# Threshold attention followed by an ELU feed-forward block: the heads of one stage in two PSUM tiles, each with its own maximum and with its bound on ScalarE

## The chip, the core and the metric

The kernel runs on one core of a Trainium2 chip. The core has five engines, each of which takes its instructions in order: TensorE (PE in the profile; its weight loads are listed apart as PEld), VectorE (DVE), ScalarE (ACT), GpSimd (POOL) and SyncE (SP, which issues the DMAs here). The metric is the device time of one execution in microseconds (us), as the median of several runs.

## The reference

Everything is float32, except that the two weight matrices arrive as 64-bit floats and are brought to 32 bits by the kernel. Cut to what matters:

```python
# q, k, v: (8, 8, 576, 64); tau = 0.02
scores = scale * np.matmul(q, k.transpose(0, 1, 3, 2))          # scale = 1/8
thresh = np.max(scores, axis=-1, keepdims=True) - tau
scores = np.where(scores >= thresh, scores, -1000000000.0)
scores = scores - np.max(scores, axis=-1, keepdims=True)
attn = np.exp(scores)
attn = attn / (np.sum(attn, axis=-1, keepdims=True) + 1e-09)
x = np.matmul(attn, v)                                          # heads side by side: (4608, 512)
h = x @ w_in                                                    # (512, 2048)
g = np.where(h > 0.0, h, np.exp(np.minimum(h, 0.0)) - 1.0)
out = g @ w_out                                                 # (2048, 512)
```

## The kernel before

**Attention in steps.** Two heads form a pair; there are 32 pairs, `pr` = 0 to 31, four to a batch. A pair is worked through in five steps, `i` = 0 to 4: steps 0 to 3 each take 128 of the 576 query rows for both heads, step 4 takes the 64 rows left over of both heads together as one tile of 128 rows ("one-head step"). Steps are counted through as n = 5 pr + i. One step consists of these parts:

- `scores` (L238): PE multiplies queries by keys into PSUM. For each half of the 576 keys (`a`) and each head (`h`) there is a matmul; the loop order is a outside, h inside. A head's scores take two PSUM banks of 288 columns each.
- `exponentials`: VectorE takes the row maximum `mx` from PSUM (L248); GpSimd makes `nb`, the maximum times minus the scale (L249), which is the bias of the exponential, and `th`, the maximum less tau in unscaled terms (L250), which is the bound below which scores are dropped; ScalarE makes `e`, the exponential of each head (L253).
- `masks` (L265): VectorE compares the scores in PSUM with `th`, multiplies by `e`, writes `w` to SBUF and sums its rows in `sm`; then it makes the reciprocals `rs` (L267, L268).
- `normalize` (L274): GpSimd multiplies `w` by `rs`.
- the turn: PE transposes `w` into PSUM (`rt`, L277) in two or three parts, and ScalarE copies them to SBUF (`wTa`, `wTb`, L293).
- `values` (L384, L388): after steps 1 and 4 of a pair, PE multiplies by v (`pv`), and ScalarE copies the result out (`xt`, L395, `xs`, L400).

**Four stages.** Steps 0 to 19 are laid out by the framework's scheduler. Steps 20 to 34 (up to `SWITCH`) have an order written out by hand, and carry beside them the conversion of the weights and the first units of the plain feed-forward block. Steps 35 to 44 (up to `MIDDLE`) run beside the rest of the plain feed-forward units, one head at a time in two PSUM tiles. From step 45 on the order comes from a planner with due times, beside a feed-forward block that needs fewer products; this stage has helpers of its own for the parts of a step: `max_of` (L1096), `bound_of` (L1100), `exp_of` (L1104, L1106), `mask_of` (L1115), `reciprocal_of` (L1121, L1122). After the last step only the feed-forward block is left.

**The stage that the change touches, steps 20 to 34.** PSUM holds three pools here: `t` with two banks (transposes and values), `f` with two banks (feed-forward) and `s` with one tile of four banks, which takes both heads of a step. The tile is given back when its masks have been made. The loop issues, in this order:

1. `scores` of step n; `values` of step n - 2 if that was a step 1 or 4 of its pair (then n mod 5 is 3 or 1; the code calls this `valued`);
2. if not `valued`: the first part of converting one weight piece (`convert_top`, two VectorE operations, L136 and L137, and `convert_add` on GpSimd, L143); the exponentials and "minus one" of feed-forward halves carried over;
3. a share of feed-forward halves on PE (`SHARES`: up to one half at each of four places), the first part of the transposes of step n - 1, and, if not `valued`, their copies on ScalarE;
4. `exponentials`; the ELU of carried halves;
5. if `valued`: `convert_top` and `convert_add` of the first piece, then the copies out of `values` and of the transposes;
6. `convert_abs` (ScalarE, L148), more feed-forward halves (L435 or L475, their exponentials L442), the second weight piece, the other transposes;
7. `masks`, "minus one" (L445), `normalize`, `convert_end` (VectorE, L155), the ELUs (VectorE, L449), and what the next pair needs (`prep_q`, L195, `copy_q`, L207, `prep_k`, L200, `copy_k`, L212, loads by SP); `convert_rest` (ScalarE, L129) of the next two pieces.

Two weight pieces are converted in each step as long as there are any. A flag, the list `apart`, tells `scores` whether the two heads share one tile or get one each; it was set after this stage.

Of the kernel before, what the change touches and what calls it, by code (L numbers as in the profile page):

```python
# [10 lines left out]
FP32 = mybir.dt.float32  # L11
U32 = mybir.dt.uint32
I32 = mybir.dt.int32
AF = mybir.ActivationFunctionType
ALU = mybir.AluOpType
AX = mybir.AxisListType
# [3 lines left out]
def kernel(  # L20
# [10 lines left out]
    nc = tc.nc  # L31
    PSUM = bass.MemoryType.PSUM
    P = 128
    B, H, S, D = q.shape
# [4 lines left out]
    HALF = S // 2  # L39
# [14 lines left out]
    att = ctx.enter_context(tc.tile_pool(name="att", bufs=2))  # L54
# [9 lines left out]
    wpool = [wstage]  # L64
# [17 lines left out]
    keep = const.tile([P, 1], FP32, name="keep")  # L82
    nc.vector.tensor_scalar(keep, pos, SCALE, None, ALU.mult)
    nkeep = const.tile([P, 1], FP32, name="nkeep")
# [3 lines left out]
    ntau = const.tile([P, 1], FP32, name="ntau")  # L88
# [129 lines left out]
    wTs, xts, open_steps, turns = {}, {}, {}, {}  # L218
    apart = []
# [24 lines left out]
    def exponentials(pr, i, hs):  # L244
        st = open_steps[pr, i]
        cs = slice(hs[0], hs[-1] + 1)
        src = st["both"] if len(hs) == 2 else st[hs[0]].unsqueeze(1)
        nc.vector.tensor_reduce(st["mx"][:, cs], src[:, :, :, :HALF], axis=AX.XY, op=ALU.max)  # L248
        nc.gpsimd.tensor_scalar(st["nb"][:, cs], st["mx"][:, cs], nkeep, 1.0, ALU.mult, ALU.mult)  # L249
        nc.gpsimd.tensor_scalar(st["th"][:, cs], st["mx"][:, cs], 1.0, ntau, ALU.mult, ALU.add)  # L250
        for h in hs:
            e = att.tile([P, 2, HALF], FP32, name="e")
            nc.scalar.activation(e, st[h][:, :, :HALF], AF.Exp, bias=st["nb"][:, h : h + 1], scale=keep)  # L253
            st[h] = st[h], e

    def masks(pr, i, hs):
        st = open_steps[pr, i]
        cs = slice(hs[0], hs[-1] + 1)
        if hs[0] == 0:
            st["w"] = wpool[0].tile([P, 2 * S], FP32, name="w")  # L260
        w, sm, rs = st["w"], st["sm"], st["rs"]
        for h in hs:
            sc, e = st.pop(h)
            wv = w[:, h * S : (h + 1) * S].rearrange("p (a n) -> p a n", a=2)
            nc.vector.scalar_tensor_tensor(wv, sc[:, :, :HALF], st["th"][:, h : h + 1], e, ALU.is_ge, ALU.mult,  # L265
                                           accum_out=sm[:, h : h + 1])
        nc.vector.tensor_scalar(sm[:, cs], sm[:, cs], 1e-9, None, ALU.add)  # L267
        nc.vector.reciprocal(rs[:, cs], sm[:, cs])  # L268

    def normalize(pr, i, hs):  # L270
        st = open_steps[pr, i]
        for h in hs:
            wv = st["w"][:, h * S : (h + 1) * S]
            nc.gpsimd.tensor_scalar(wv, wv, st["rs"][:, h : h + 1], 1.0, ALU.mult, ALU.mult)  # L274

    def transpose(dst, src):
        nc.tensor.matmul(dst, src, ident, is_transpose=True, skip_group_check=True)  # L277
# [228 lines left out]
    def heads_of(i):  # L506
        return [0, 1] if i < NC else [0]
# [68 lines left out]
        if hs == [1]:  # L576
            ahead(pr, i + 1)
    first.close()
    for name, bufs in (("s", 1), ("f", 2)):
        psum[name] = banks.enter_context(tc.tile_pool(name=f"ps_{name}", bufs=bufs, space=PSUM))  # L580

    while len(turned) > 1:
# [8 lines left out]
    with tc.manual_schedule():  # L591
        carried = []
        for _ in range(2):
            load_w(4)
        for n in range(per_seq, SWITCH):
            pr, i = step = steps[n]
            hs = heads_of(i)
            now = range(progress[1], min(progress[1] + 2, len(pieces)))
            if n == per_seq:
                for x in now:  # L600
                    convert_rest(x)
            for _ in now:
                load_w(4)
            scores(*step, hs)
            valued = steps[n - 2][1] in (1, NB - 1)
            if valued:
                out_values = values(steps[n - 2][0], 0 if steps[n - 2][1] == 1 else 1)
            parts = turn_parts(*steps[n - 1])

            if not valued:  # L610
                for x in now[:1]:
                    convert_top(x)
            finish_units(carried, slice(0, 2))
            if not valued:
                for x in now[:1]:
                    convert_add(x)
            share = SHARES[n % NB]
            early_ = ffn_halves(share[0])
            copies = parts[0]()
            if not valued:  # L620
                copies()
            exponentials(*step, hs)
            finish_units(carried, slice(2, None))
            if valued:
                for x in now[:1]:
                    convert_top(x)
                    convert_add(x)
            if valued:
                out_values()
                copies()  # L630
            for x in now[:1]:
                convert_abs(x)
            finish_units(early_, ACT)
            after = ffn_halves(share[1])
            finish_units(after, ACT)
            after = early_ + after
            for x in now[1:]:
                convert_top(x)
                convert_add(x)
                convert_abs(x)  # L640
            parts[1]()()
            second = ffn_halves(share[2])
            finish_units(second, ACT)
            if len(parts) > 2:
                parts[2]()()
            carried = ffn_halves(share[3])
            masks(*step, hs)
            finish_units(after, slice(1, 2))
            normalize(*step, hs)
            finish_units(second, slice(1, 2))  # L650
            for x in now:
                convert_end(x)
            finish_units(after + second, slice(2, None))
            if i in (2, 3):
                (prep_q if i == 2 else prep_k)(pr + 1)
                (copy_q if i == 2 else copy_k)(pr + 1)
            if i in (3, 4):
                load(pr + 2, ("qm",) if i == 3 else ("km",))
            if i == 3:
                load(pr + 1, ("v",))  # L660
            if steps[n - 2] == (NPAIR - 1, NB - 1):
                push_ffn(0)
            for x in range(progress[1], min(progress[1] + 2, progress[0])):
                convert_rest(x)
        finish_units(carried, ALL)
        turn(*steps[SWITCH - 1])
        finish_units(ffn_halves(len(pending)), ALL)
        behind(*steps[SWITCH - 2])
        behind(*steps[SWITCH - 1])
    assert progress[1] == len(pieces)  # L670
    assert units[0][1][0] == 1 and not pending
    banks.close()
    apart.append(True)
    for name, bufs, stack in (("f", 3, ctx), ("s", 2, banks), ("t", 1, banks)):
        psum[name] = stack.enter_context(tc.tile_pool(name=f"ps_{name}2", bufs=bufs, space=PSUM))
    early.close()
# [80 lines left out]
    with tc.manual_schedule():  # L757
        after = []
        make_out(1), make_out(0)
        for n in range(SWITCH, MIDDLE):  # L760
            pr, i = steps[n]
            hs = heads_of(i)
# [328 lines left out]
                    at(end + lag, f)  # L1091
                n -= 1

        def max_of(pr, i, h):
            st = open_steps[pr, i]
            nc.vector.tensor_reduce(st["mx"][:, h : h + 1], st[h][:, :, :HALF], axis=AX.XY, op=ALU.max)  # L1096

        def bound_of(pr, i, h):
            st = open_steps[pr, i]
            nc.gpsimd.tensor_scalar(st["th"][:, h : h + 1], st["mx"][:, h : h + 1], 1.0, ntau, ALU.mult, ALU.add)  # L1100

        def exp_of(pr, i, h):
            st = open_steps[pr, i]
            nc.scalar.mul(st["nb"][:, h : h + 1], st["mx"][:, h : h + 1], nkeep)  # L1104
            e = att.tile([P, 2, HALF], FP32, name="e")
            nc.scalar.activation(e, st[h][:, :, :HALF], AF.Exp, bias=st["nb"][:, h : h + 1], scale=keep)  # L1106
            st[h] = st[h], e

        def mask_of(pr, i, h):
            st = open_steps[pr, i]  # L1110
            if h == 0:
                st["w"] = wpool[0].tile([P, 2 * S], FP32, name="w")
            sc, e = st.pop(h)
            wv = st["w"][:, h * S : (h + 1) * S].rearrange("p (a n) -> p a n", a=2)
            nc.vector.scalar_tensor_tensor(wv, sc[:, :, :HALF], st["th"][:, h : h + 1], e, ALU.is_ge, ALU.mult,  # L1115
                                           accum_out=st["sm"][:, h : h + 1])

        def reciprocal_of(pr, i, hs):
            st = open_steps[pr, i]
            cs = slice(hs[0], hs[-1] + 1)  # L1120
            nc.vector.tensor_scalar(st["sm"][:, cs], st["sm"][:, cs], 1e-9, None, ALU.add)  # L1121
            nc.vector.reciprocal(st["rs"][:, cs], st["sm"][:, cs])  # L1122

        begun = [0.0]

        def softmax(pr, i):
# [40 lines left out]
        for n in range(MIDDLE, len(steps) + 3):  # L1167
            pr, i = divmod(n, NB)
# [61 lines left out]
        w = wpool[0].tile([P, 2 * S], FP32, name="w")  # L1230
# [8 lines left out]
        a, z = B - 1, B  # L1239
# [45 lines left out]
```

## Time and profile before

| what | value |
|---|---|
| median of 6 runs | 1377.13 us (1375.71 to 1379.39) |
| the profiled execution: its time | 1375.71 us |
| its span, first to last instruction | 1373.9 us |
| mean granted clock of TensorE | 0.992 |
| busy in the span: PE, DVE, POOL, ACT | 97%, 77%, 61%, 46% |
| instructions | 21955 |

A busy time is the time in which the engine had an instruction in work. "Idle before" and the waits are attributed to the instruction that came last of those waited for. Windows are given in us from the start of the span; for each the profile lists the busy time of PE, PEld, DVE, ACT and POOL with the number of instructions, the clock that TensorE was granted as a share of full speed, and the share and rate of the DMA engines. The chain of waits is the work that ended last, followed back from the end: each line gives a start, a duration, and the engine and group, and "issue" is time for which the profile shows no wait.

### The profile page before, as it was taken

What the parts mean: (1) busy time and instruction counts of PE and PEld (TensorE: products, weight loads), DVE (VectorE), ACT (ScalarE), POOL (GpSimd) and SP (SyncE); (2) the same over time, 40 slices, a digit from 0 to 9 for tenths busy, and PEclk for the clock granted to TensorE, in tenths of its full rate; (3) what the DMA queues carried; (4) which work ended last, traced back from release to release, by engine and by line L of the source; (5) the groups of instructions that cost most, each with busy time, mean ns of one, the idle gap of its engine ahead of it and who ended that gap; (6) DMA issues with size and microseconds to landing.
All of it is one profiled execution on the core that took longest, in us unless ns stands there. A gap on an engine that the chain in (4) does not pass through costs nothing.

```text
span 1373.9 us, 21955 instructions
## 1 busy us (share of the span) xinstructions
PE 1331.8 (97%) x6566; PEld 990.1 (72%) x6566; DVE 1060.9 (77%) x2364; ACT 625.3 (46%) x1371; POOL 835.0 (61%) x1345
## 2 busy tenths in 40 slices
PE   6898989999999999999999999999999999999998
PEld 4555745746777777777777777777777777888886
DVE  6778895888879887988799878988888875545433
ACT  4666664225454454545353636364535442312320
POOL 5567774778657574757476747665575646525423
PEclk9999999999999999999999999999999999999999
DMA  5235452589798989898889889897989785321211
GB/s 116 58 84 148 143 145 47 167 241 264 222 244 231 281 218 256 226 263 233 235 234 262 243 232 255 224 260 212 246 230 278 223 241 165 124 68 66 93 58 31
DMA packets 316342, 259.82 MB, mean 189 GB/s; under 512 B 208320, under 2 KB 272320, under 8 KB 316224
## 3 DMA queue, kind: packets, MB, share of 16 engines
q1 hardware_dynamic: 316224, 258.42, 68.0%
q8 instruction: 53, 0.87, 0.3%
q14 instruction: 65, 0.53, 0.1%
HBM read 167.84 MB, written 90.51 MB: 188 GB/s over the span
## 4 chain that ended last, share of the span: by engine, by line
PE 87%; DVE 5%; POOL 2%; ACT 2%; issue 2%; DMA 1%; SPq 1%; DVEq 0%; POOLq 0%; ACTq 0%
PE f L1012 28%; PE f L857 28%; PE sc L238 13%; PE pv L388 9%; PE f L475 3%; PE pv L384 3%; PE f L435 3%; PE rt L277 1%; DVE w L265 1%; ACT e L253 1%; DVE mx L248 1%; POOL wtop L143 1%; POOL w L274 1%; DVE wtop L136 0%; DVE wtop L137 0%
## 5 line engine op out<-in xcount | busy, mean ns | idle before, releaser
L274 POOL TENSOR_SCALAR w<-w,rs 128x576 f32<-128x576 f32 x288 | 247.7, 866 | 108.2 <-DVE rs L1122 74.8
L1096 DVE TENSOR_REDUCE mx<-sc 128x1 f32<-128x576 f32 x207 | 148.0, 752 | 80.6 <-PE sc L238 80.5
L238 PE MATMUL sc<-kT,qT 64*128 64x288 f32 x1024 | 182.4, 440 | 26.8 <-DVE w L265 17.2
L348 DVE STREAM_TRANSPOSE x<-w 128x512 f32<-128x512 f32 (+1 forms) x350 | 182.6, 568 | 8.2 <-POOL w L274 8.2
L1106 ACT ACTIVATE e<-sc,nb,keep 128x576 f32<-128x576 f32 x207 | 172.2, 832 | 6.9
L1115 DVE SCALAR_TENSOR_TENSOR w<-sc,th,e 128x576 f32<-128x576 f32 x207 | 163.2, 811 | 8.5 <-ACT e L1106 0.4
L1104 ACT ACTIVATE nb<-mx,nkeep 128x1 f32<-128x1 f32 x207 | 61.5, 297 | 232.0 <-DVE mx L1096 232.0
L238 PEld LDWEIGHTS sc<-kT,qT 64*128 64x128 f32 x1024 | 100.5, 190 | 91.9 <-issue 52.7
L857 PE MATMUL f<-xt,sw 128*128 128x256 f32 x512 | 128.9, 389 | 0.5 <-DVE g L879 0.5
L857 PE MATMUL f<-xt,w_in_sb 128*128 128x256 f32 x512 | 124.5, 382 | 0.3 <-ACT w L871 0.2
L1100 POOL TENSOR_SCALAR th<-mx,ntau 128x1 f32<-128x1 f32 x207 | 54.7, 266 | 104.7 <-DVE mx L1096 104.4
L857 PEld LDWEIGHTS f<-xt,sw 128*128 128x128 f32 x512 | 93.3, 190 | 29.0 <-issue 13.5
L857 PEld LDWEIGHTS f<-xt,w_in_sb 128*128 128x128 f32 x512 | 96.1, 190 | 18.9 <-ACT xs L400 4.6
L1012 PE MATMUL f<-w_out_sb,s 128*128 128x256 f32 x448 | 109.4, 387 | 0.0
L1012 PE MATMUL f<-w_out_sb,g 128*128 128x256 f32 x448 | 107.5, 382 | 0.5 <-DVE g L912 0.5
L253 ACT ACTIVATE e<-sc,nb,keep 128x576 f32<-128x576 f32 x81 | 65.2, 831 | 92.1 <-POOL nb L249 91.1
L1012 PE MATMUL f<-t,s 128*128 128x256 f32 x448 | 106.6, 380 | 0.3 <-POOL s L949 0.3
L857 PE MATMUL f<-x,w_in_sb 128*128 128x256 f32 x448 | 105.8, 379 | 0.0
L1012 PEld LDWEIGHTS f<-w_out_sb,s 128*128 128x128 f32 x448 | 82.3, 190 | 23.0 <-issue 11.6
L1012 PEld LDWEIGHTS f<-w_out_sb,g 128*128 128x128 f32 x448 | 83.8, 190 | 16.8 <-issue 3.8
L876 POOL TENSOR_TENSOR u<-u,w 128x256 f32<-128x256 f32 x64 | 49.1, 767 | 76.4 <-ACT u L871 76.4
L1012 PEld LDWEIGHTS f<-t,s 128*128 128x128 f32 x448 | 84.1, 190 | 13.7 <-POOL s L949 2.7
(162 smaller groups left out, 2579.3 us busy)
## 6 DMA issues: line engine op xcount, KB each, us to landing
there<-x SPq DMA_DIRECT2D x500, 144.0 KB, 4.3
wTb<-there SPq DMA_DIRECT2D x75, 576.0 KB, 4.8
wTa<-there SPq DMA_DIRECT2D x50, 576.0 KB, 4.4
sw<-win_sums SPq DMA_DIRECT2D x62, 384.0 KB, 4.7
t<-wout_sums SPq DMA_DIRECT2D x45, 512.0 KB, 5.4
qm<-in_q_dram SPq DMA_DIRECT2D x128, 72.0 KB, 4.4
vm<-in_v_dram SPq DMA_DIRECT2D x64, 128.0 KB, 4.3
wst<-in_moe_w_in_dram SPq DMA_DIRECT2D x16, 512.0 KB, 4.5
```

The costliest lines, as they stand in the source:

```text
L238: nc.tensor.matmul(scs[h][:, a, :HALF], qs[r], kT[r, k0 : k0 + HALF], start=True, stop=True)
L253: nc.scalar.activation(e, st[h][:, :, :HALF], AF.Exp, bias=st["nb"][:, h : h + 1], scale=keep)
L274: nc.gpsimd.tensor_scalar(wv, wv, st["rs"][:, h : h + 1], 1.0, ALU.mult, ALU.mult)
L348: nc.vector.transpose(x[:, :, c0 : c0 + nc_], src.rearrange("p (c g n) -> p g c n", c=nc_, n=T))
L388: nc.tensor.matmul(pv[h * D : (h + 1) * D, g0 * T : g1 * T], vm[:, h, c], wT[:, g0:g1, h * (NC + 1) + c], start=False, stop=(c == NC - 1), ...
L857: nc.tensor.matmul(loc["banks"][place], left[:, j], right[:, j], start=(begins and j == 0), stop=(j == 1), skip_group_check=True)
L1012: nc.tensor.matmul(place(m), lhs, rhs, start=(begins and v == 0), stop=(v == RU - 1), skip_group_check=True)
L1096: nc.vector.tensor_reduce(st["mx"][:, h : h + 1], st[h][:, :, :HALF], axis=AX.XY, op=ALU.max)
L1100: nc.gpsimd.tensor_scalar(st["th"][:, h : h + 1], st["mx"][:, h : h + 1], 1.0, ntau, ALU.mult, ALU.add)
L1104: nc.scalar.mul(st["nb"][:, h : h + 1], st["mx"][:, h : h + 1], nkeep)
L1106: nc.scalar.activation(e, st[h][:, :, :HALF], AF.Exp, bias=st["nb"][:, h : h + 1], scale=keep)
L1115: nc.vector.scalar_tensor_tensor(wv, sc[:, :, :HALF], st["th"][:, h : h + 1], e, ALU.is_ge, ALU.mult, accum_out=st["sm"][:, h : h + 1])
```

## The change

In steps 20 to 34 each head gets a PSUM tile of its own: the pool `s` has two tiles of two banks instead of one of four, and the flag `apart` is set ahead of the stage. `exponentials` is replaced there by the three helpers of the last stage, called head by head: a maximum per head on VectorE, `nb` per head on ScalarE right ahead of that head's exponential, and `th` per head on GpSimd. `masks` is replaced by `mask_of` for each head and one `reciprocal_of`. The helpers are moved up in the file so that both stages can call them. The places of the parts in the loop stay as they were, and the stages behind are as they were.

```diff
+    def max_of(pr, i, h):
+        st = open_steps[pr, i]
+        nc.vector.tensor_reduce(st["mx"][:, h : h + 1], st[h][:, :, :HALF], axis=AX.XY, op=ALU.max)
+
+    def bound_of(pr, i, h):
+        st = open_steps[pr, i]
+        nc.gpsimd.tensor_scalar(st["th"][:, h : h + 1], st["mx"][:, h : h + 1], 1.0, ntau, ALU.mult, ALU.add)
+
+    def exp_of(pr, i, h):
+        st = open_steps[pr, i]
+        nc.scalar.mul(st["nb"][:, h : h + 1], st["mx"][:, h : h + 1], nkeep)
+        e = att.tile([P, 2, HALF], FP32, name="e")
+        nc.scalar.activation(e, st[h][:, :, :HALF], AF.Exp, bias=st["nb"][:, h : h + 1], scale=keep)
+        st[h] = st[h], e
+
+    def mask_of(pr, i, h):
+        st = open_steps[pr, i]
+        if h == 0:
+            st["w"] = wpool[0].tile([P, 2 * S], FP32, name="w")
+        sc, e = st.pop(h)
+        wv = st["w"][:, h * S : (h + 1) * S].rearrange("p (a n) -> p a n", a=2)
+        nc.vector.scalar_tensor_tensor(wv, sc[:, :, :HALF], st["th"][:, h : h + 1], e, ALU.is_ge, ALU.mult,
+                                       accum_out=st["sm"][:, h : h + 1])
+
+    def reciprocal_of(pr, i, hs):
...
     first.close()
-    for name, bufs in (("s", 1), ("f", 2)):
+    apart.append(True)
+    for name, bufs in (("s", 2), ("f", 2)):
         psum[name] = banks.enter_context(tc.tile_pool(name=f"ps_{name}", bufs=bufs, space=PSUM))
...
-            exponentials(*step, hs)
+            for h in hs:
+                max_of(pr, i, h)
+                exp_of(pr, i, h)
+                bound_of(pr, i, h)
             finish_units(carried, slice(2, None))
...
-            masks(*step, hs)
+            for h in hs:
+                mask_of(pr, i, h)
+            reciprocal_of(pr, i, hs)
             finish_units(after, slice(1, 2))
             normalize(*step, hs)
...
     banks.close()
-    apart.append(True)
```

More of the change, by code (lines that the diff above doesn't have):

```diff
@@ L274, in normalize @@
             nc.gpsimd.tensor_scalar(wv, wv, st["rs"][:, h : h + 1], 1.0, ALU.mult, ALU.mult)
+    def max_of(pr, i, h):
[19 more added lines that the diff above has]
+    def reciprocal_of(pr, i, hs):
+        st = open_steps[pr, i]
+        cs = slice(hs[0], hs[-1] + 1)
+        nc.vector.tensor_scalar(st["sm"][:, cs], st["sm"][:, cs], 1e-9, None, ALU.add)
+        nc.vector.reciprocal(st["rs"][:, cs], st["sm"][:, cs])
     def transpose(dst, src):
@@ L1092, in ffn_quarters @@
                 n -= 1
[L1094 to L1122, printed above, removed]
         begun = [0.0]
```

## The prediction

> **What bounds the kernel now.** I read the whole span first, then the stage that is edited, then the single steps of it. All times are from the profiled execution of the kernel before (span 1373.9 us). Table of windows over the stage, its parts and what follows (us of the window, then the busy time of each engine, the granted clock, DMA share):
>
> ```profile
> 157.80:166.70 8.90, 8.90 (x54) 5.92 (x53) 8.76 (x17) 6.28 (x14) 6.02 (x7) 1.00 0.37 123
> 192.00:201.40 9.40, 6.46 (x25) 2.93 (x24) 8.01 (x16) 6.97 (x16) 6.43 (x6) 1.00 0.49 125
> 201.40:212.00 10.60, 10.59 (x45) 5.00 (x45) 10.17 (x19) 5.52 (x11) 8.76 (x8) 0.84 0.30 103
> 240.20:1300.00 1059.80, 1056.52 (x5252) 804.61 (x5251) 848.62 (x1898) 470.80 (x1059) 661.83 (x1075) 1.00 0.78 218
> ```
>
> Behind 240.2 PE idles 3.3 us in 1060: what is saved ahead of it should move the rest as a block. The edited stage (steps 20 to 34, from 105.9 to 240.2) has PE busy 118.2 of 134.3, so 16 us of gaps, spread unevenly: some steps are full (157.8), others wait (192.0). At most these 16 us and the time lost to the halved clock are to be had. The waits of that stage say for whom (us in total, times, longest):
>
> ```profile
> ACT e L253 <- POOL nb L249: 27.0, 13, 3.9
> PE sc L238 <- DVE w L265: 13.5, 7, 4.5
> DVE w L265 <- ACT e L253: 13.3, 10, 2.8
> ```
>
> PE's scores wait for the masks (w), the masks for the exponentials (e), these for the bound nb on GpSimd. The chain of waits through step 30 shows how (start, us, engine, group):
>
> ```profile
> 196.28 1.29 POOL wtop L143
> 197.58 0.43 POOL nb L249
> 198.01 0.02 issue
> 198.03 0.62 ACT e L253
> ...
> 198.76 0.83 ACT e L253
> ...
> 199.70 1.57 DVE w L265 x4
> 201.27 0.14 issue
> 201.41 1.24 PE sc L238 x8
> ```
>
> The maxima (L248) had begun at 195.97 and taken 1.35, so they were ready at 197.3, but nb stands in GpSimd's queue behind a weight conversion (wtop L143), then both exponentials run, and only then both masks, since both heads lie in one tile.
>
> **The change part by part.** *Maxima.* One reduce of 1152 columns (mean 1342 ns, 11 rows) becomes two of 576, which the last stage has already (L1096, median 749 ns, a pair back to back 1.40 to 1.42 us). So +0.07 us of DVE for each of the 12 two-head steps, but the first maximum stands 0.6 us earlier. [...]
>
> *Bound nb.* It leaves GpSimd (266 to 450 ns a step, behind L143) for ACT, one per head (L1104, median 295 ns, with the exponential 0.3 us after nb's start: 340.67 to 340.99). ACT takes +0.6 us per two-head step; it is busy 78.6 of 134.3. Behind the two nb on ACT are queued weight absolutes, transposed copies and the FFN's exponentials; they start no later as long as the exponentials end no later. With GpSimd free, before: reduce 1.35, nb 0.4, two exponentials 1.55, some 3.4 us from the first reduce's start; after: 0.75 + 0.3 + 0.83 + 0.3 + 0.83, about 3.1. The lower bound th stays on GpSimd, two small ops for one; in step 30 the first would come at 197.6 and end by 198.3 even at the 0.73 of the contended rows, before its mask wants it.
>
> *Masks, scores, order.* Mask 0 needs only exponential 0, and the next step's head-0 scores only mask 0. In the trace the two heads' matmuls of a step overlap (eight passes of 0.40 in 1.24 us); what head 0 gains by going ahead I price at nothing, since PE stands in order and head 1 still needs its 1.24 us after mask 1. It costs nothing either, as PE idles there. No DMA and no instruction of SP moves.
>
> Now the steps. Steps count i = n mod 5; i = 0, 2, 4 convert the first weight piece ahead of the maxima, i = 1, 3 both pieces between maxima and masks.
>
> Two-head steps that convert first (20, 22, 25, 27, 30): from the reduce's start to the first mask 125.23 to 128.95, 152.18 to 155.91, 171.36 to 175.09, 195.97 to 199.70: 3.73 each. After: the DVE's own queue decides, 1.42 for the pair, 1.34 for the second conversion (L136, L137: 172.63 to 173.97), then the mask: 2.8. Exponential 0 is ready after 0.75 + 0.05 + 0.3 + 0.83 = 1.9, th after some 2.3. Gain 0.9 each. Steps 21, 23, 28, 31 (i = 1, 3): the masks follow two conversions on DVE at once (120.18, 137.80), not the exponentials; the pair costs 0.07 to 0.1 there. Steps 24, 29 (one head): mask after DVE's conversion instead of after nb, 0.4 earlier (146.2 for 146.58; 191.7 for 192.10).
>
> Following the start of the next step's scores, with what each step passes on:
> - Step 20: +0.9. Step 21: reduce waited for the scores until 115.65; head 0 done first lets it start some 0.5 earlier, minus 0.1: 1.3 in all.
> - Step 22: +0.9, PE's own work fits (7.6 of 8.8): 2.2. Step 23: -0.1, 2.1. Step 24: +0.4, 2.5.
> - Steps 25, 26: PE waits for an ELU (L449) to 149.97, which hangs on step 24's mask, and is then busy without a gap to 166.7. Nothing added: 2.5 on PE; but the masks of 26 come 3.1 to 3.4 early.
> - Step 27: chain of normalize (L274), L445, ELU, conversion, reduce, all behind mask 26: 3.1 + 0.9 = 4.0. Step 28: -0.1. Step 29: PE full, its 0.4 stays on DVE: 3.9.
> - Step 30: 0.4 + 0.9: 5.2.
> - Step 31: the clock, next paragraph: 1.65, 6.85.
> - Step 32: exponentials wait for a PSUM copy on ACT (215.56, 0.59), so 0.3 + 0.83 + 0.3 + 0.83 follow where 1.55 did; mask 0 goes with exponential 0, and the two cancel: 0. Steps 33, 34: PE full (20.86 of 20.9): 0.
>
> *Clock.* Two halved stretches lie in the stage; windows cut at their edges:
>
> ```profile
> 107.40:110.81 3.41, 1.46 (x10) 0.82 (x7) 2.38 (x3) 1.51 (x4) 1.26 (x4) 0.99 0.87 292
> 110.81:114.22 3.41, 0.90 (x4) 0.82 (x6) 2.55 (x8) 3.39 (x8) 1.67 (x2) 0.50 0.02 8
> ...
> 172.25:175.66 3.41, 2.04 (x7) 0.76 (x5) 2.27 (x4) 2.24 (x4) 3.15 (x4) 1.00 0.00 0
> 175.66:179.07 3.41, 2.36 (x16) 1.41 (x18) 3.34 (x10) 2.70 (x6) 2.47 (x3) 1.00 0.08 18
> 199.56:202.97 3.41, 1.56 (x9) 1.07 (x10) 3.21 (x9) 2.77 (x8) 1.68 (x2) 0.99 0.01 2
> 202.97:206.38 3.41, 3.41 (x12) 1.25 (x12) 3.34 (x5) 1.55 (x2) 3.30 (x5) 0.51 0.83 291
> ```
>
> With PE busy 1.46 and 1.56 the next window ran at half clock, with 2.04 at full clock. The halving after 202.97 cost 0.45 on L384 (1.36 for 0.91) and 1.20 on L388 (3.57 for 2.37): 1.65 us, on a step where PE is full. Step 30's gap of 2.9 us shrinks to about 1.4, so no window holds less than some 2.0 of work, and the halving should go. The first halving begins before the change has acted; I leave it. [...]
>
> Sum: 6.85 us off this execution's 1375.71 (span plus 1.8 us around it), 1368.9. That execution is the fastest of the six, 1.4 below the median of 1377.13; off the median, 1370.3.
>
> **The rivals.** *The second half gives nothing back* (time 1374.6): behind step 25 PE is full, and in step 27 normalize and L445 (166.77 to 169.66) stand on the path. If they don't come earlier, and the clock still halves, only the 2.5 of steps 20 to 24 stays. Against: both hang on mask 26. *The bounds sit on ACT's path* (slower, 1381.6): where a copy from PSUM holds ACT until after the maximum, as in step 32, the two nb add 0.6 us between copy and last exponential; if in all 12 two-head steps one nb (0.30) and the reduce's 0.07 land on the path, 12 x 0.37 = 4.4 us. It decides once copies end later than the first maximum in most steps; for: ACT executes in order; against: in step 30 the copy ends at 197.26, 0.5 after the first maximum would, and the mask is held longer by DVE. *No change* (1377.1): scores still wait for both heads and DVE's queue, 8.76 busy of 8.9 in step 26, decides everywhere. Against: DVE idles 13.3 us for the exponentials.
>
> **How the numbers follow.** Forecast 0.70 (own range 1368 to 1373), second half lost 0.14, no change 0.06, slower 0.10. A measurement here can tell about 0.2%, 2.75 us: faster is below 1374.4. The forecast is faster throughout but for 0.01; the half gain is split, 0.09 to 0.05. So faster 0.78, same 0.12, slower 0.10. Range: from 1367.0 (if also the first halving ends a window sooner) to 1377.0, which leaves out the slow rival and some of the edges.
>
> **What would show it.** L249's wait gone, e waiting for DVE's maxima instead; reduce to first mask 2.8 in steps 22, 25, 27, 30; scores of step 35 at 233 instead of 240.2; clock 1.00 in step 31; stage idle of PE near 10. Wrong, if step 35 begins at 240, or if it begins early and the span does not follow.

## The result and the profile after

The changed kernel takes 1372.91 us (median of 25 runs, 1369.76 to 1381.02), the kernel before 1377.45 us (median of 50): a ratio of 0.9964, 95% interval 0.9955 to 0.9974, so 3.6 to 6.2 us off. The forecast was 6.85 us off, and faster. Two later comparisons of the same two kernels gave 0.9969 (0.9958 to 0.9980) and 0.9976 (0.9961 to 0.9991).

The two profiled executions alone don't show this: their spans are 1373.9 and 1373.8 us, although the scores of step 35 begin at 234.93 us instead of 240.19 (forecast 233); 0.9 us of that stand ahead of the stage, whose scores of step 20 end at 107.19 for 108.05. An early step 35 that the span does not follow was one of the prediction's two signs of being wrong, so the executions have to be cut at the stage. The windows that answer to those shown of before, with the step's own bounds (step 26; step 30; step 31; then two parts of the rest):

```profile
155.63:164.53 8.90, 8.90 (x52) 5.92 (x51) 8.50 (x17) 6.57 (x14) 5.88 (x8) 1.00 0.33 123
188.65:195.49 6.84, 5.62 (x23) 2.98 (x23) 6.70 (x15) 4.86 (x12) 5.49 (x6) 1.00 0.55 164
195.49:206.73 11.24, 11.22 (x44) 5.12 (x44) 10.87 (x22) 7.58 (x18) 9.40 (x9) 0.85 0.26 96
352.00:620.00 268.00, 263.84 (x1343) 198.98 (x1343) 224.92 (x519) 123.84 (x279) 164.32 (x278) 1.00 0.87 238
620.00:1300.00 680.00, 679.18 (x3404) 530.40 (x3401) 522.05 (x1164) 300.57 (x687) 405.73 (x654) 1.00 0.74 208
```

Step 26 is as full as before. Step 30 has lost much of its gap: PE idles 1.2 us in it for 2.9 (compare the idle times, not the lengths, since the window shown of before began 1 us ahead of the step's scores). In the whole stage PE idles 7.3 us (105.01 to 234.93) for 16.1. Step 31 still has a clock of 0.85. And PE idles 4.2 us between 352 and 620, where before it idled 0.5 in the same stretch of work (357 to 625): that is where this one execution gave most of its gain back, see the repeated profiles below. The waits of the stage:

```profile
ACT nb L286 <- DVE mx L278: 9.3, 9, 2.2
DVE w L297 <- ACT e L288: 5.0, 7, 3.1
PE sc L238 <- DVE w L297: 4.9, 5, 2.6
```

The wait of ACT for nb on GpSimd (27.0 us) is gone; ACT waits 9.3 us for the maxima instead. DVE waits 5.0 us for exponentials (13.3 before), PE 4.9 us for masks (13.5 before). The chain through step 30, which went through GpSimd and both exponentials, now stays on DVE:

```profile
191.39 0.69 DVE wtop L137
192.08 1.33 DVE mx L278 x2
193.41 0.49 DVE wtop L136
193.90 0.02 issue
193.92 0.21 DVE wtop L137
194.13 0.40 issue
194.53 0.65 DVE w L297
...
195.49 0.72 PE sc L238 x2
196.21 0.02 issue
196.23 1.21 PE sc L238 x6
```

From the reduce's start (192.00 in the timeline) to the first mask are 2.53 us, for 3.73 before. PE's scores come in two pieces, two passes after mask 0, six after mask 1.

Step by step, the time from the end of the scores of step n to the end of those of step n + 1, worked out from the rows of L238, in two profiles of before and four of the changed kernel:

| n | before | before again | changed | 2nd | 3rd | 4th |
|---|---|---|---|---|---|---|
| 20 | 7.56 | 7.55 | 6.10 | 6.71 | 6.11 | 6.70 |
| 21 | 7.42 | 7.42 | 8.89 | 7.31 | 8.88 | 7.39 |
| 22 | 8.78 | 8.78 | 7.53 | 7.54 | 7.54 | 7.53 |
| 23 | 8.83 | 8.84 | 8.48 | 8.47 | 8.48 | 8.47 |
| 24 | 8.06 | 8.05 | 8.05 | 8.01 | 8.04 | 8.03 |
| 25 | 10.32 | 10.31 | 10.62 | 12.32 | 10.63 | 12.32 |
| 26 | 8.91 | 8.91 | 8.91 | 8.91 | 8.91 | 8.91 |
| 27 | 10.02 | 10.01 | 8.27 | 8.27 | 8.27 | 8.27 |
| 28 | 8.85 | 8.83 | 8.54 | 8.54 | 8.54 | 8.53 |
| 29 | 7.43 | 7.43 | 7.40 | 7.41 | 7.41 | 7.41 |
| 30 | 8.42 | 8.41 | 7.45 | 7.45 | 7.46 | 7.45 |
| 31 | 10.53 | 10.53 | 10.53 | 10.53 | 10.53 | 10.53 |
| 32 to 34 | 28.25 | 28.24 | 28.20 | 28.19 | 28.20 | 28.20 |
| 20 to 34 | 133.37 | 133.31 | 128.98 | 129.65 | 129.00 | 129.74 |
| step 35 to the end | 1132.50 | 1133.79 | 1137.64 | 1131.64 | 1132.79 | 1134.44 |

The stage gains 3.6 to 4.4 us, 4.0 in the mean. What lies behind it differs by 6 us among executions of one kernel.

### The profile page after: what moved, and what is told of

Read it like the earlier page. It is cut to its first block, busy times and chain, and to the rows that moved or that the text cites. A ratio compares the mean times of both kernels' runs of the same rounds, so it can differ in the third digit from the quotient of the medians.

```text
span 1373.8 us, 22005 instructions
## 1 busy us (share of the span) xinstructions
PE 1336.0 (97%) x6566; PEld 991.4 (72%) x6566; DVE 1061.7 (77%) x2376; ACT 633.4 (46%) x1398; POOL 831.6 (61%) x1342
## 4 chain that ended last, share of the span: by engine, by line
PE 84%; DVE 6%; ACT 3%; DMA 2%; POOL 2%; issue 2%; SPq 1%; DVEq 0%; POOLq 0%; ACTq 0%
PE f L892 27%; PE f L1047 27%; PE sc L238 12%; PE pv L418 9%; PE f L505 3%; PE pv L414 3%; PE f L465 2%; PE rt L307 2%; ACT e L288 1%; DVE w L297 1%; DMA wTa<-there 1%; POOL w L274 1%; DVE w L265 1%; DVE mx L278 1%; DMA there<-x 1%
## 5 line engine op out<-in xcount | busy, mean ns | idle before, releaser
L278 DVE TENSOR_REDUCE mx<-sc 128x1 f32<-128x576 f32 x234 | 167.1, 751 | 89.9 <-PE sc L238 89.9
L238 PE MATMUL sc<-kT,qT 64*128 64x288 f32 x1024 | 184.9, 438 | 18.4 <-DVE kT L200 8.6
L288 ACT ACTIVATE e<-sc,nb,keep 128x576 f32<-128x576 f32 x234 | 194.7, 832 | 7.9
L297 DVE SCALAR_TENSOR_TENSOR w<-sc,th,e 128x576 f32<-128x576 f32 x234 | 184.5, 811 | 15.4 <-ACT e L288 5.4
L286 ACT ACTIVATE nb<-mx,nkeep 128x1 f32<-128x1 f32 x234 | 69.3, 296 | 241.1 <-DVE mx L278 241.1
L238 PEld LDWEIGHTS sc<-kT,qT 64*128 64x128 f32 x1024 | 101.6, 189 | 84.9 <-issue 51.2
L282 POOL TENSOR_SCALAR th<-mx,ntau 128x1 f32<-128x1 f32 x234 | 67.8, 291 | 114.6 <-DVE mx L278 114.2
L892 PEld LDWEIGHTS f<-xt,sw 128*128 128x128 f32 x512 | 93.3, 190 | 29.0 <-issue 13.5
L892 PEld LDWEIGHTS f<-x,w_in_sb 128*128 128x128 f32 x448 | 85.1, 190 | 11.6
```

Source lines behind the costliest of these rows:

```text
L238: nc.tensor.matmul(scs[h][:, a, :HALF], qs[r], kT[r, k0 : k0 + HALF], start=True, stop=True)
L892: nc.tensor.matmul(loc["banks"][place], left[:, j], right[:, j], start=(begins and j == 0), stop=(j == 1), skip_group_check=True)
```

## The experiments

**The changed kernel again, three more profiles.** No edit.

> The changed kernel itself, profiled a second time. My theory: the stage of steps 20 to 34 gains about 4.4 us in every execution, and the 5 us that the profiled execution gave back between steps 49 and 87 were waits of values on fetched transposes, which differ from execution to execution. It expects step 35 about 4 to 6 us earlier than before, and a stretch from step 35 to the end between 1132 and 1138 us, shorter than the 1138.9 of the first profile; time ratio 0.995 to 0.998. The rival, that an earlier start collides with the transfers behind and gives most of it back for good, expects about 1139 us from step 35 to the end again.

> The changed kernel, profiled a third time. My theory: the same steps as in the two profiles before (22, 23, 27, 28, 30 within 0.1 us), while the halved stretches fall where the windows of 3.41 us happen to lie; the stretch from step 35 to the end between 1131 and 1138 us.

> The changed kernel beside the filled ones on one chip. My theory: step 31 at 10.5 again and the kernel with four gaps filled 2 to 3 us faster; ratio against before 0.996 to 0.9975.

The steps 22, 23, 27, 28 and 30 came out as in the first profile within 0.02 us, the rest of the program at 1131.6, 1132.8 and 1134.4 (1137.6 in the first; the expectations count from the start of step 35's scores, 1.2 us earlier). In the first profile PE had these waits from 314 to 680 us (total, times, longest):

```profile
PE pv L414 <- DMA wTa<-there: 1.8, 2, 1.4
PE pv L414 <- issue: 1.7, 1, 1.7
PE pv L414 <- DMA there<-x: 1.2, 2, 0.7
```

These are `values` waiting for transposes that come back by DMA, 4.7 us in all (for the wait under "issue" the profile shows no releaser; it stands ahead of the same `values`, and that it is a DMA's too is inferred). The second profile has none for a DMA there. So the rival falls: an earlier start does not meet a collision that returns the gain; the waits come and go with the execution (4.7 us in the first, none in the second, 1.0 and 1.6 in the third and fourth, those under "issue" counted in). The mean stage gain of the four profiles, 4.0 us, lies inside the interval of each of the three ratios.

**The kernel before again.** No edit.

> The kernel before, profiled a second time. My theory: steps 22 to 30 as in its first profile within 0.1 us, unless a halved stretch falls into one; step 31 halved again (10.5); from step 35 to the end 1131 to 1138 us, by the execution and not by the kernel.

As expected; step 31 again took 10.53.

**Two tiles alone.** Each head has its tile and its maximum, but nb stays on GpSimd:

```diff
             for h in hs:
-                max_of(pr, i, h)
-                exp_of(pr, i, h)
-                bound_of(pr, i, h)
+                exponentials(pr, i, [h])
```

> The heads in two PSUM tiles with a maximum each, but the bound nb left on GpSimd (per head). My theory (both parts are needed): the first mask may go after the first exponential, but nb still queues behind the weight conversion, so reduce to first mask is about 3.0 us in steps 22, 25, 27, 30 (before 3.73, after 2.5), the second mask ends about 0.4 us earlier than before where after gains 0.9 to 1.2; one-head steps 24 and 29 gain nothing; stage gain 1.5 to 2.5 us, ratio 0.998 to 0.999. The rival that only the freed GpSimd queue counts expects no gain here (within 0.5 us of before).

Reduce to first mask was 3.00 us in steps 22, 25, 27 and 30, to the last mask's end 4.78 (before 5.28, changed 4.08 in 25, 27, 30); one-head steps unchanged at 3.00. The stage took 131.27, 2.1 less than before, but that is no measure of the tiles' worth: step 20 alone took 2.5 less (5.02), while steps 30 and 31, with a halved clock from 197.53 to 204.36, were longer than before (8.90 and 11.15). The ratio was 0.9974 (0.9964 to 0.9984), better than expected, and not told apart from the changed kernel's 0.9969 measured beside it. DVE's timeline in step 30:

```profile
192.57 1.41 DVE L248 TENSOR_REDUCE mx<-sc 128x1 f32<-128x576 f32 x2
193.90 0.56 DVE L136 TENSOR_SCALAR wtop<-wst 128x512 uint32<-128x512 uint32 x1
194.49 0.69 DVE L137 SCALAR_TENSOR_TENSOR wtop<-wst,wtop 128x512 uint32<-128x512 uint32 x1
195.57 0.82 DVE L297 SCALAR_TENSOR_TENSOR w<-sc,th,e 128x576 f32<-128x576 f32 x1 [0.38 <-POOL nb L249]
```

The first mask starts 3.00 after the reduce. The row names nb on GpSimd; on ACT the first exponential ran from 194.62 to 195.45, 0.12 ahead of the mask, and it came late, since its nb (194.14) stood behind the conversion on GpSimd (192.89, 1.29 us).

**The bound alone.** nb on ScalarE per head, but one tile and one maximum for both heads, from the kernel before:

```diff
-        nc.gpsimd.tensor_scalar(st["nb"][:, cs], st["mx"][:, cs], nkeep, 1.0, ALU.mult, ALU.mult)
+        if not on_act:
+            nc.gpsimd.tensor_scalar(st["nb"][:, cs], st["mx"][:, cs], nkeep, 1.0, ALU.mult, ALU.mult)
...
         for h in hs:
+            if on_act:
+                nc.scalar.mul(st["nb"][:, h : h + 1], st["mx"][:, h : h + 1], nkeep)
             e = att.tile([P, 2, HALF], FP32, name="e")
...
-            exponentials(*step, hs)
+            exponentials(*step, hs, on_act=True)
```

> The bound nb moved to ScalarE, one per head ahead of its exponential, but both heads left in one PSUM tile with one maximum. My theory: nb no longer waits for the conversion on GpSimd, but both masks wait for the second exponential, which ends 1.35 + 0.3 + 0.83 + 0.3 + 0.83 = 3.6 us after the reduce begins, where before it ended at 3.6: reduce to first mask 3.7, no gain in two-head steps, 0.4 in the one-head steps 24 and 29; stage gain 0 to 1 us, ratio 0.999 to 1.0005. The rival that the queue of GpSimd was the whole cause expects 3 us or more of the 4.4.

Reduce to first mask 3.70 in steps 22, 25 and 27, 2.53 in the one-head steps, as expected. The time was 1.0015 (1.0002 to 1.0028) of the kernel before, its interval reaching just into the 0.9990 to 1.0005 expected. The stage took 135.08, 1.7 more than before, as much as step 32 took more (9.10 for 7.40). There the two nb and two exponentials follow a copy out of PSUM on ACT (218.53, 0.58 us), and both masks wait for the last (220.39, 0.83 us); reduce to first mask rose from 4.50 to 5.14, and the longer gap of PE was followed by a halved clock at 222.8, in which the scores of step 33 took 2.29 us for 1.24. The slow rival of the prediction was real at the one place that it named. In step 30 DVE shows the wait that the second tile removes:

```profile
198.87 1.35 DVE L248 TENSOR_REDUCE mx<-sc 128x2 f32<-128x1152 f32 x1
200.14 0.63 DVE L136 TENSOR_SCALAR wtop<-wst 128x512 uint32<-128x512 uint32 x1
200.80 0.69 DVE L137 SCALAR_TENSOR_TENSOR wtop<-wst,wtop 128x512 uint32<-128x512 uint32 x1
202.66 0.82 DVE L268 SCALAR_TENSOR_TENSOR w<-sc,th,e 128x576 f32<-128x576 f32 x1 [1.17 <-ACT e L256]
```

DVE is done with the conversion by 201.5 and waits 1.17 us for an exponential; on ACT the first had started at 200.68 and taken 0.83, so it is the second that ends last. So neither part alone makes the chain as short as both do (3.00, 3.70 and 2.53 us), and in two-head steps the tiles bring the larger share. In the measured time only the tiles' gain shows: that nb on ACT adds to it is shown in the chain alone.

**Head 1 first on PE.** In the scores of steps 20 to 34 the loop over heads runs backwards, so no matmul goes ahead of the last mask:

```diff
-            for h in hs:
+            for h in order or hs:
...
-            scores(*step, hs)
+            scores(*step, hs, hs[::-1])
```

> As changed, but PE takes head 1 ahead of head 0 in the scores of steps 20 to 34, so that no matmul of a step goes before the last mask of the step before. My theory priced head 0 going ahead at nothing: stage gain as in the changed kernel within 0.7 us, ratio within 0.001 of it. The rival, that starting with head 0 is where part of the gain comes from, expects 1 us or more less. A second rival: without the early pair PE has its work in one piece, and whether the clock is halved in steps 20, 21 and 31 changes with it; then the rows of those steps differ by the halved clock's 1.6 to 3.9 us.

> Head 1 first on PE, profiled a second time. My theory: which side of the halving step 31 falls on is decided by where the windows of 3.41 us lie in the execution, so step 31 is 8.9 or 10.5, and the other steps as in its first profile; the rival, that the order of the heads keeps the clock, expects 8.9 again for any place of the windows.

The ratio was 0.9972 (0.9959 to 0.9985) beside 0.9969 of the changed kernel: head 0 going ahead is worth nothing that shows. The stage took 127.4 in both profiles, less than the changed kernel's by more than the 0.7 expected. The steps 22 to 30 are within 0.15 us of the changed kernel (step 25 of the two profiles that were halved there), but step 20 was 5.59, for 6.10 to 6.71, and step 31 was 8.89 in both profiles, for 10.53 in all four of the changed kernel. Its clock was not halved there:

```profile
195.41:198.82 3.41, 2.50 (x10) 1.27 (x10) 3.34 (x10) 3.35 (x8) 2.78 (x3) 1.00 0.01 5
198.82:202.24 3.42, 3.42 (x23) 1.78 (x23) 3.35 (x6) 2.93 (x8) 3.42 (x5) 1.00 0.91 303
```

The same two windows of the changed kernel (first profile), with the clock halved:

```profile
194.18:197.60 3.42, 2.18 (x10) 1.23 (x10) 3.35 (x10) 3.36 (x9) 2.79 (x3) 1.00 0.12 49
197.60:201.01 3.41, 3.41 (x12) 1.15 (x13) 3.34 (x7) 2.49 (x5) 3.41 (x5) 0.50 0.75 280
```

Whether the order of the heads or the place of the windows did it can't be read from this pair: the windows' edges stand elsewhere too (0.47 and 0.62 us after the end of step 31's scores, 0.13 to 0.39 in the four of the changed kernel). The account of step 31 below comes back to it.

**Gaps of PE filled.** Matmuls of 128 x 512 whose product nobody reads, in the changed kernel:

```diff
+    def keep_warm(k):
+        if k:
+            idle = psum["t"].tile([P, 512], FP32, name="idle", tag="rt")
+            for _ in range(k):
+                nc.tensor.matmul(idle, ident, w_in_sb[:, 0, :512], start=True, stop=True, skip_group_check=True)
...
             carried = ffn_halves(share[3])
+            keep_warm({30: 1}.get(n, 0))
```

> As changed, plus one matmul of 128 x 512 between the last feed-forward half of step 30 and the scores of step 31; its product is not used. It fills about 0.9 of the 1.2 us that PE waits there for mask 0. My theory: the 1.65 us that the prediction counted for step 31 did not come because the clock was still halved there (in both profiles of the changed kernel, windows with PE busy 2.2 of 3.4), so with the gap filled step 31 takes 8.9 us instead of 10.5 from scores to scores, and the time falls by about 1.6 us more, ratio 0.995 against before. The rival, that step 31 is bound by something else (DVE behind the scores), expects 10.5 again and no gain.

> One matmul at the end of step 30, profiled a second time. My theory: step 31 at 8.9 again, since the filled gap leaves no window in which PE has little work. The rival, that the first profile of it only met a lucky place of the windows, expects 10.5 in some executions.

Step 31 was 8.89 us in both profiles, 1.64 less than unfilled: the price of the halving in the prediction, 1.65, was right. But the edges stood at 0.49 and 0.56 us behind the scores, as in the runs with head 1 first, which kept the clock unfilled; this run alone does not show that filling did it. The time, 0.9967 (0.9951 to 0.9983), does not differ measurably from the changed kernel's.

With three at the end of step 20, one behind the scores of step 25 and one at the end of step 30:

> As changed, plus unused matmuls of 128 x 512 in three gaps of PE: three at the end of step 20, one behind the scores of step 25, one at the end of step 30. My theory: the halved clock of steps 21, 25 and 31 goes; steps 20 and 21 together 12.5 to 13.5 us instead of 14.0 to 15.0, step 25 at 10.3 in every execution, step 31 at 8.9; stage about 126 us, ratio 0.993 to 0.995. The rival, that the clock matters only in step 31 because DVE decides in the other two, expects no more than the kernel with the one matmul.

Steps 25 and 31 took 10.63 and 8.89; the first halving went, but another came from 120.66 to 124.08, over the end of step 21 and the start of step 22 (8.39 and 8.44). The stage took 127.14 (126 expected), the ratio was 0.9958 (0.9944 to 0.9971), a smaller gain than the 0.993 to 0.995 expected. With two at the end of step 20, two at the end of step 21, and the others as before:

> As the kernel with unused matmuls in three gaps, but two instead of three at the end of step 20 and two more at the end of step 21, whose gap had halved step 22 there. My theory: no halved stretch from step 20 to 35; steps 20 and 21 together about 13.2 us, step 22 at 7.5, step 25 at 10.6, step 31 at 8.9; stage about 126 us, 3 us less than the changed kernel in this call. The rival, that the windows fall so that some gap halves the clock all the same, expects 127 to 129.

No halving in the whole stage. Step 22 was 7.54, 25 10.63, 31 8.89; step 21, where the fillers themselves hold the scores up, 9.30. The stage took 127.13, 2.6 less than the changed kernel's 129.74 measured beside it, not the 126 expected. The windows around step 30's end:

```profile
193.51:196.92 3.41, 3.14 (x13) 1.38 (x12) 3.34 (x9) 3.35 (x9) 2.78 (x3) 1.00 0.17 67
196.92:200.34 3.42, 3.42 (x22) 1.63 (x22) 3.35 (x7) 2.91 (x7) 3.42 (x5) 1.00 0.73 285
```

Here the edge (placed by continuing the 3.41 us grid from this execution's halving at 63.8) stands 0.15 us behind the scores of step 31, as in two profiles of the changed kernel (0.16 and 0.13), and the clock stayed at 1.00 where it was halved there. So at this place of the windows the filling kept the clock, in this one execution. In the time nothing of it is certain: 0.9963 (0.9951 to 0.9975) beside 0.9976 (0.9961 to 0.9991) of the changed kernel on the same chip, medians 1372.76 and 1372.42. No version tried is shown to beat the changed kernel.

## Why the prediction was right, and where it was not

The direction, the range and the mechanism held; the sum was 6.85, the stage gave 3.6 to 4.4 in the profiles. By its steps:

- *Reduce to first mask.* Forecast 2.8 for 3.73; measured 2.53 in steps 25, 27 and 30 of the first profile (2.73 in step 22, 2.86 in step 20). The working added up whole durations, whose tails overlap: the pair of reduces holds DVE 1.33, not 1.42, and the conversion some 1.2, not 1.34. Step 22 gained 1.25 (forecast 0.9); 27 gained 1.75 (forecast 1.5: 4.0 less the 2.5 that PE had); 30 gained 0.97 (forecast 1.3).
- *Both parts are needed.* The prediction gave the masks' freedom to the tiles and nb to ACT; the two partial kernels show 3.00 and 3.70 us from reduce to first mask for them, where both give 2.53.
- *Steps 23 and 28.* Forecast -0.1 each, for the longer pair. Measured gains of 0.35 and 0.3. Reduce to first mask is 4.40 for 4.48, so the pair costs nothing there; where the other 0.2 come from was not tried.
- *Steps 24 and 29.* The mask came 0.47 earlier behind the reduce, as forecast (0.4), but the steps stayed at 8.0 and 7.4: PE is full in both (8.03 of 8.05 and 7.40 of 7.40). The prediction had said this of 29 alone. Its cost: 0.4.
- *Steps 20 and 21.* Forecast 1.3 together; measured 0.0 or 0.9. The prediction left the first halving as it was, but at the same length it now covers other work. In the first profile it ran from 112.26 to 119.09, over the values of step 21, whose 16 matmuls (L418) took 4.48 us for 2.58 before.
- *Step 25.* Forecast nothing; measured a loss of 0.3, and of 2.0 in two of four profiles, where the clock was halved in it.
- *Step 31, the clock.* This is the step that failed: 1.65 forecast, nothing measured in four profiles. The price was right, the condition was not. The prediction took PE's busy time in a window as the sign, halved at 1.5, kept at 2.0, and reckoned that a gap of 1.4 us leaves 2.0. The gap did shrink, to 1.22 us between transposes and scores, and the window held 2.18 busy, and was halved. Busy time in this view is a union of intervals in which a matmul was in work; scores that wait between their two pieces, and that use 64 rows, count in full. Windows with less, such as 1.95 in step 25 of the first profile (146.40 to 149.81), kept the clock.

  The traces hold a sign that does tell the windows apart, found afterwards and tried by no run of its own. Count for each matmul record of PE in a window (in part at the edges) its columns, times the share of the 128 rows that it uses: 144 for a pass of scores, 288 columns on 64 rows. Then the window ahead of step 31's halving held 1330 and 1260 in the two profiles of before, and 1300, 1360, 1300 and 1460 in the four of the changed kernel: the eight passes of scores (1152) and a piece of the `values`. The shorter gap stretched the scores over more time (the eight passes took 1.94 us, 195.49 to 197.43, for 1.24 before) and added no work. With the grid laid by each execution's last halving ahead of 1300 us, all 40 windows at full clock that a halving followed, from 36 to 1300 us in all fourteen traces, count 1472 at most, and all 5060 others 1561 at least, while by busy time the two kinds overlap (up to 2.44 halved, from 1.74 kept). The margin is thin: a grid moved by 0.08 us makes the two ranges overlap.

  By this sign the place of the windows was enough in the kernel with head 1 first (1740 and 1590) and in that with the one matmul (1690 and 1630 with the unused matmul left out of the count), and the filling was needed in the last one (2420, and 1390 with it left out).
- *The rest of the program.* It follows the stage as a block in the mean, as forecast: 1134.1 us over four profiles, 1133.1 over two of before, a difference far inside the 6 us between executions. That one execution can give back 5 us in DMA waits was not foreseen; it does not show in the ratio.
- *The rivals.* "The second half gives nothing back" fell: steps 27 to 30 gain 3.0. "No change" fell: the interval of each ratio ends below 1. "ACT's path" was met at step 32 only in the kernel with the bound alone.

## What to carry to other kernels

A one-column value made by another engine came here only after what stood ahead of it in that engine's queue: in step 30 of the kernel before, the maxima were ready at 197.3, and nb began on GpSimd at 197.58, behind a conversion of 1.29 us. A 0.3 us operation (median 0.295 us on ACT) moved to the engine that needs it, and a shared tile split so that each half is freed by its own reader, took 1.2 us out of a chain (3.73 to 2.53), and neither did so alone (3.70 and 3.00). Before adding up such a chain, ask for each step whether PE or the chain ends last, and count only the latter; price a clock effect apart, with its own chance, since here it went by windows whose place differed between executions of one program (the first halving of the stage began 2.5 to 5.1 us after the same scores), and don't take a shorter gap for more work in the window (ahead of step 31 a gap of 1.2 us for 2.9 left 1300 by the count above, for 1330). If two profiles don't show what the medians show, cut both at the stage's end and compare the parts.

## What the runs showed of the hardware that was not expected

- In all fourteen traces the halved clock comes, ahead of 1300 us, in multiples of 3.41 us (in the first profile of before 10.24 from 62.96, 6.83 from 110.75 and 3.41 from 202.91; in the first of the changed kernel 6.83 from 64.47, 6.83 from 112.26 and 3.41 from 197.60), on a grid whose place differs between executions of one program: the first halving of the stage began 5.1, 2.5, 5.1 and 2.7 us after the end of step 20's scores in the four profiles of the changed kernel, and with that steps 21 and 25 change by 1.5 to 1.7 us each.
- A window with PE busy 2.18 of 3.41 us was followed by half clock, one with 1.95 in the same execution was not. Counted as columns times the share of 128 rows in use, the first held 1300 and the second 2070; the line between halved and kept lies between 1472 and 1561 in the fourteen traces.
- From step 45 to step 90 the changed kernel took 325.5 to 331.4 us in its four profiles; from step 90 to step 159 all of them took 496.9 to 497.5.
